# Other slots for the weight preparation inside an attention loop: offsets 0, 14, 23 in place of 0, 10, 18

## The chip, the core and the metric

The kernel runs on one core of a Trainium2 chip: TensorE (PE; its weight loads are told apart as PEld), VectorE (DVE), ScalarE (ACT), GpSimd (POOL) and SyncE (SP), which here issues nearly all DMAs. Time is device time in microseconds (us). The kernel before takes 1760.26 us, the median of three runs (1758.9 to 1764.62).

## The reference

It is one transformer block, whose inputs and outputs are float32. Its attention reads a cache; only the last 512 of the cached keys count.

```python
h = _layernorm(x) * (1 + ca) + sa                    # x: 2048 x 512
q = h @ wq                                           # 32 heads of 128
scores = q k^T * Dh ** -0.5                          # 8 kv heads, last 512 keys
x = x + ga * (softmax(scores) @ v) @ wo
h = _layernorm(x) * (1 + cb) + sb
x = x + gb * ((_gelu(h @ w_gate) * (h @ w_up)) @ w_down)   # F = 1792
```

## The kernel before

**Arithmetic.** Each float32 operand is split into two float16 halves, a high and a low part, and a product is three matmuls (`mm3`, lines 85 to 87: high by high, high by low, low by high). The projections and the feed-forward products (FFN) use seven block products in place of eight, so their weights are needed as sums and differences of blocks too, each again split in two halves.

**The loop.** The attention is one loop over T = 512 slots, written out in Python. A slot t is one scoring tile of 128 rows by 512 keys. Four slots are a unit (one head on one block of 512 rows). In slot t the program writes down, in this order: the three scoring matmuls of tile t on PE (`scores`, into one of two banks `ps`); the row maximum on DVE (`peak`, L943, `nm<-ps`); the low half of the probabilities of tile t-3 on DVE (`low`, L971) with their DMA transpose on SP (L975, `pt<-p`); the exponential of tile t on ACT (`expo`, L952, `ee<-ps,nm`); the high half of tile t-2 on ACT (L966); then about three groups of matmuls of other work (query projection `qa`, `qb`, `qc`, probabilities by values `po`, output projection `py`). All engines keep this written order: nothing is reordered by a scheduler. Since there are two `ps` banks, the scoring matmuls of tile t wait for the exponential of tile t-2.

**The weight preparation.** At the end of a slot stands what a table of positions puts there. In the second half of the loop this is, among other things, the preparation of the FFN weights, in seven rounds n = 0 to 6 of 30 slots each, which begin at slot b = 286 + 30 n. A round is for a pair of FFN tiles and has three parts:

- `prep_set(2n, b)` for the gate weights and `prep_set(2n+1, ...)` for the up weights. Each loads two tiles of float32 weights (`rw<-in_wg`, `rw<-in_wu`); at offsets 1 and 2 from the part's begin ACT takes their sums of squares (`sumsq`, L216, `junk<-rw`); at offset 4 a small matmul (L220) and a chain of column operations make a scale from them (`f_spread`); at offsets 7, 9, 10, 11 and 12 POOL scales the tiles, makes the sums and differences, and splits them into staging tiles (L160, L156, L157, L1360), and SP stores each three slots after (`kept<-stage`).
- `prep_wd(n, ...)` for the down weights, in the same way: loads `raw<-in_wd`, sums of squares at its offsets 0 and 1, the scale at 4, POOL's work at 7, 9, 11, 12 and 13 (L156, L157, L1413; DVE scales first, L1410), stores three slots after.

**Buffers and loads.** The `rw` tiles have two buffers, the `raw` and staging tiles five together. A planner goes through all loads in order of their first use. It wants a load three slots before that use (AHEAD), but not before the buffer that it takes is free by the table (its last use plus one slot), and if that is later than the use itself, it puts the load into the slot of the use:

```python
go = pos[0] - ahead
free = released[kind].pop(0) + LDGAP
pending[kind].append((max(min(max(go, free), pos[0]), 0), max(free + 3, pos[0] - 9), load))
```

SP issues in the written order. A load whose buffer is still being read waits on SP, and what stands behind it on SP waits too.

Of the kernel before, what the change touches and what calls it, by code (L numbers as in the profile page):

```python
# [62 lines left out]
def block_kernel(ctx: ExitStack, tc: tile.TileContext, x, kT, v, wq, wo, wg, wu, wd, cT, wc, wm, out):  # L63
# [11 lines left out]
    def raw(name):  # L75
        return pool.tile([P, 512], F32, tag="raw", name=name, bufs=NRAW)
# [14 lines left out]
    def dma(out_, in_):  # L91
        moved[0] += 1
        nc.sync.dma_start(out_, in_)
# [58 lines left out]
    def halves(dst, src, act=False):  # L152
        if act:
            nc.scalar.activation(dst[:, 0, :], src, AF.Copy)
        else:
            nc.gpsimd.tensor_scalar(dst[:, 0, :], src, 1.0, 1.0, op0=ALU.mult, op1=ALU.mult)  # L156
        nc.gpsimd.tensor_tensor(dst[:, 1, :], src, dst[:, 0, :], op=ALU.subtract)  # L157

    def times(t, by):
        nc.gpsimd.tensor_scalar(t, t, by, 1.0, op0=ALU.mult, op1=ALU.mult)  # L160
# [15 lines left out]
    def col(name, i=0):  # L176
        return ST[name][:, i:i + 1]
# [7 lines left out]
    def little(name, n=1, bufs=4, dtype=F32):  # L185
        return small.tile([P, n], dtype, tag=name, name=name, bufs=bufs)
# [27 lines left out]
    def sumsq(out, src):  # L214
        with nc.allow_low_precision(reason="only a scale follows from it, which the margin in norm2 covers"):
            nc.scalar.activation(junk, src, AF.Square, scale=PRE, accum_out=out)  # L216
# [75 lines left out]
    def f_spread(i, m):  # L292
        w = little("lw", 1, 2)
        norm2(w, m, 2, 1.0 / TOP13)
        pool_ts(col("finv", i), w, col("mf"))
        pool_ts(col("tsc", i), col("finv", i), GELU_A * GELU_C)
        then(lambda: nc.vector.reciprocal(col("fsc", i), w))
# [24 lines left out]
    def store(key, t, slack=6):  # L322

        KEPT[key] = dram.tile(list(t.shape), F16, name="kept")
        if slack and 0 <= now[0] < T - 8:
            bg.append((now[0] + slack, now[0], len(KEPT), lambda: dma(KEPT[key], t)))
        else:
            dma(KEPT[key], t)
# [225 lines left out]
    def sched(pos, ld, *more, kind="raw", ahead=AHEAD, lane="w"):  # L554
        loads.append(((pos,) + more, ld, kind, ahead, lane))
# [164 lines left out]
    def set_load(key, srcs, only=None):  # L720
        for k, src in enumerate(srcs):
            if only in (None, k):
                t = pool.tile([P, 512], F32, tag="rw", name="rw", bufs=NRW)
                dma(t, src)
                RAW.setdefault(key, {})[k] = t

    def pair_stat(key, m, k):
        if not m:
            m["m"] = little("lm", 4, dtype=BF16)
        sumsq(m["m"][:, k:k + 1], RAW[key][k])  # L730
# [35 lines left out]
    def plain_steps(key, by):  # L766
        def part(k):
            SET.setdefault(key, [None, None])[k] = get_w(k)
            times(RAW[key][k], by)
            halves(SET[key][k], RAW[key][k])  # L770

        return lambda: part(0), lambda: part(1)
# [386 lines left out]
    for g in range(NG):  # L1159
# [6 lines left out]
        if 0 < g < GW:  # L1166
            a, b = plain_steps(g, by)
            sched_pair(g, srcs, t0 - (19 if g > 1 else 13), spread, [(t0 - (13 if g > 1 else 8), a)], [(t0 - (11 if g > 1 else 7), b)])
        elif g >= GW and (not half or pr < GW):
            sched_set(g, srcs, t0, by, spread)  # L1170
            if not half:
                a, b, c, d, e, f = SETPOS2 if g == GW else SETPOS
# [32 lines left out]
    def set_srcs(q):  # L1205
        n, m = divmod(q, 2)
        f = 2 * (n % NP)
        return [(wg, wu)[m][f], (wg, wu)[m][f + 1]]

    def f_scale(q):  # L1210
        return (q // 2) % NP * 2 + q % 2
# [133 lines left out]
    def staged():  # L1345
        box = {}

        def alloc():
            box["t"] = pool.tile([P, 2, 512], F16, tag="raw", name="stage", bufs=NRAW)

        return box, alloc

    def prep_set(q, b):
        m, key, by = {}, ("f", q), col("fsc", f_scale(q))
        l, r = slice(0, 256), slice(256, 512)
        outs = [staged() for _ in range(4)]
        srcs = set_srcs(q)

        def tt(o, a, c, op):
            nc.gpsimd.tensor_tensor(o, a, c, op=op)  # L1360

        def made(k, src):
            halves(outs[k][0]["t"] if k < 3 else outs[k][0]["t"][:, :, 0:256], src)

        def keep_it(k):
            return lambda: store(("w", key, k), outs[k][0]["t"] if k < 3 else outs[k][0]["t"][:, :, 0:256], 0)

        def s0():
            times(RAW[key][0], by)
            made(0, RAW[key][0])  # L1370

        def s1():
            r1 = RAW[key][1]
            times(r1, by)
            made(3, r1[:, r])
            tt(r1[:, r], r1[:, l], r1[:, r], ALU.add)

        def s2():
            r0, r1 = RAW[key][0], RAW[key][1]
            tt(r1[:, l], r0[:, l], r1[:, l], ALU.subtract)  # L1380
            tt(r0[:, l], r1[:, r], r0[:, l], ALU.subtract)
            tt(r0[:, r], r0[:, r], r0[:, l], ALU.subtract)

        sched(b + 1, (lambda: set_load(key, srcs, 0), [lambda: pair_stat(key, m, 0), nop]), b + 11, kind="rw")
        sched(b + 2, (lambda: set_load(key, srcs, 1), [lambda: pair_stat(key, m, 1), lambda: f_spread(f_scale(q), m["m"]), s2, nop]),
              b + 4, b + 10, b + 12, kind="rw")
        sched(b + 7, (outs[0][1], [s0, keep_it(0)]), b + 10)
        sched(b + 9, (outs[3][1], [s1, keep_it(3)]), b + 12)
        sched(b + 11, (outs[1][1], [lambda: made(1, RAW[key][0]), keep_it(1)]), b + 14)
        sched(b + 12, (outs[2][1], [lambda: made(2, RAW[key][1]), keep_it(2)]), b + 15)  # L1390

    def prep_wd(n, b):
        m, st = {}, {}
        outs = [staged() for _ in range(4)]
        l, r = slice(0, 256), slice(256, 512)

        def load(k):
            st[k] = raw("raw")
            dma(st[k], wd[(2 * n + k) * P:(2 * n + k + 1) * P, :])

        def stat(k):
            if not m:
                m["m"] = little("lm", 4, dtype=BF16)
            sumsq(m["m"][:, k:k + 1], st[k])

        def spread():
            d_spread(n, m["m"])

        def scaled(k):
            nc.vector.scalar_tensor_tensor(st[k], st[k], col("dsc", n), rows[5], op0=ALU.mult, op1=ALU.mult)  # L1410

        def minus(o, a, b):
            nc.gpsimd.tensor_tensor(st[o[0]][:, o[1]], st[a[0]][:, a[1]], st[b[0]][:, b[1]], op=ALU.subtract)  # L1413

        def more():
            st[2] = raw("raw")

        def s0():
            scaled(0)
            halves(outs[0][0]["t"], st[0])  # L1420

        def s1():
            scaled(1)
            halves(outs[1][0]["t"], st[1])

        def s2():
            minus((2, l), (1, r), (1, l))
            minus((2, r), (0, r), (2, l))
            minus((0, r), (0, r), (1, r))
            minus((0, l), (0, l), (2, r))  # L1430

        def keep_it(k):
            return lambda: store(("wd", n, k), outs[k][0]["t"], 0)

        sched(b, (lambda: load(0), [lambda: stat(0), nop]), b + 13)
        sched(b + 1, (lambda: load(1), [lambda: stat(1), spread, nop]), b + 4, b + 11)
        sched(b + 7, (outs[0][1], [s0, keep_it(0)]), b + 10)
        sched(b + 9, (outs[1][1], [s1, keep_it(1)]), b + 12)
        if n < NP - 1:
            sched(b + 11, (more, [s2, nop]), b + 13)  # L1440
            sched(b + 12, (outs[2][1], [lambda: halves(outs[2][0]["t"], st[2]), keep_it(2)]), b + 15)
            sched(b + 13, (outs[3][1], [lambda: halves(outs[3][0]["t"], st[0]), keep_it(3)]), b + 16)

    at(T // 2 + 34, lambda: mod_row(5))
    for n in range(NP):
        b = T // 2 + 30 + 30 * n
        prep_set(2 * n, b)
        prep_set(2 * n + 1, b + 10)
        prep_wd(n, b + 18)
    for k in range(2):  # L1450
        at(T - 1 + 2 * k, lambda k=k: WO.update({("f", 0, k): fetch(("wd", 0, k), get_wo())}))
    for q, ps_ in ((0, (T - 18, T - 17, T - 16, T - 15)), (1, (T - 8, T - 7, T - 3, T)), (2, (T + 2, T + 3, T + 4, T + 5))):
# [242 lines left out]
    for i in range(QT):  # L1695
        load, stat, norm, sub, alloc, high, low, turn = ln_pair(3, i, lambda k, i=i: y1_row(2 * QT + QT * k + i))
        b = 26 + 16 * i
# [16 lines left out]
    for q in range(NQ):  # L1714
        n, m = divmod(q, 2)
# [54 lines left out]
```

## Time and profile before

| | us |
|---|---|
| median of three runs (lowest, highest) | 1760.26 (1758.9, 1764.62) |
| the profiled execution | 1758.56 |
| its span, first to last instruction | 1756.8 |
| busy PE, DVE, ACT, POOL | 1715.1, 1485.1, 1218.3, 1001.9 |

The granted TensorE clock is 0.996 of full speed over the span. A matmul of 512 columns is drawn 0.38 us long, but the next one starts 0.22 us after it, since matmuls overlap; a loss on PE is therefore read from starts. The attention loop runs from about 24 us to about 1340 us of the span, and rounds 0 to 6 of the weight preparation from about 742 us to about 1300 us.

### The profile page before, as it was taken

What the parts mean: (1) busy time and instruction counts of PE and PEld (TensorE: products, weight loads), DVE (VectorE), ACT (ScalarE), POOL (GpSimd) and SP (SyncE); (2) the same over time, 40 slices, a digit from 0 to 9 for tenths busy, and PEclk for the clock granted to TensorE, in tenths of its full rate; (3) what the DMA queues carried; (4) which work ended last, traced back from release to release, by engine and by line L of the source; (5) the groups of instructions that cost most, each with busy time, mean ns of one, the idle gap of its engine ahead of it and who ended that gap; (6) DMA issues with size and microseconds to landing.
All of it is one profiled execution on the core that took longest, in us unless ns stands there. A gap on an engine that the chain in (4) does not pass through costs nothing.

```text
span 1756.8 us, 26455 instructions
## 1 busy us (share of the span) xinstructions
PE 1715.1 (98%) x8264; PEld 810.2 (46%) x8266; DVE 1485.1 (85%) x2552; ACT 1218.3 (69%) x2731; POOL 1001.9 (57%) x1210
## 2 busy tenths in 40 slices
PE   7999999999999999999999999999999999999998
PEld 4444444444444444444444434444444444445556
DVE  8888898989999898988897978889786688878776
ACT  6987888888878777778777777778775244445542
POOL 3999668787887834547476566467521432214431
PEclk9999999999999999999999999999999999999999
DMA  6989999999999988999999999899997444454331
GB/s 211 231 189 224 214 230 212 233 218 213 228 206 235 228 187 177 201 196 220 204 229 198 232 184 221 197 206 223 210 211 175 162 126 127 116 167 145 105 123 49
DMA packets 698349, 336.56 MB, mean 192 GB/s; under 512 B 597473, under 2 KB 612065, under 8 KB 698209
## 3 DMA queue, kind: packets, MB, share of 16 engines
q1 hardware_dynamic: 697920, 334.36, 84.1%
q8 instruction: 65, 1.06, 0.3%
q14 instruction: 76, 0.61, 0.1%
q10 hardware_dynamic: 288, 0.52, 0.1%
HBM read 132.78 MB, written 56.75 MB: 108 GB/s over the span
## 4 chain that ended last, share of the span: by engine, by line
PE 80%; DVE 9%; DMA 3%; ACT 3%; POOL 3%; issue 2%; SPq 1%; POOLq 0%; ACTq 0%; DVEq 0%
PE py L87 6%; PE py L86 6%; PE py L85 6%; PE ps L85 5%; PE ps L87 5%; PE ps L86 5%; PE po L87 5%; PE po L85 5%; PE po L86 5%; PE fa L85 3%; PE fa L87 3%; PE fa L86 3%; PE qa L85 2%; PE qa L87 2%; DVE p L971 2%; PE qa L86 2%
## 5 line engine op out<-in xcount | busy, mean ns | idle before, releaser
L952 ACT ACTIVATE ee<-ps,nm 128x512 f32<-128x512 f32 x512 | 350.3, 684 | 237.0 <-DVE nm L943 233.4
L971 DVE SCALAR_TENSOR_TENSOR p<-ee,rr,p 128x512 f16<-128x512 f32 x512 | 457.5, 894 | 21.0 <-ACT p L966 20.6
L943 DVE TENSOR_REDUCE nm<-ps 128x1 f32<-128x512 f32 x512 | 350.1, 684 | 108.6 <-PE ps L87 105.8
L966 ACT ACTIVATE p<-ee,rr 128x512 f16<-128x512 f32 x512 | 362.7, 709 | 1.8 <-DMA pt<-p 1.8
L85 PE MATMUL ps<-k,qt 128*128 128x512 f16 x512 | 194.4, 380 | 22.1 <-ACT ee L952 21.1
L85 PE MATMUL po<-pt,v 128*128 128x512 f16 x512 | 194.1, 379 | 3.8 <-DMA pt<-p 3.1
L87 PE MATMUL ps<-k,qt 128*128 128x512 f16 x512 | 194.8, 381 | 0.6 <-DVE qt L682 0.6
L87 PE MATMUL po<-pt,v 128*128 128x512 f16 x512 | 194.2, 379 | 0.9 <-POOL v L157 0.8
L86 PE MATMUL ps<-k,qt 128*128 128x512 f16 x512 | 194.8, 380 | 0.0
L87 PE MATMUL py<-wo,ot 128*128 128x512 f16 x512 | 194.2, 379 | 0.0
L86 PE MATMUL py<-wo,ot 128*128 128x512 f16 x512 | 194.2, 379 | 0.0
L86 PE MATMUL po<-pt,v 128*128 128x512 f16 x512 | 194.2, 379 | 0.0
L85 PE MATMUL py<-wo,ot 128*128 128x512 f16 x512 | 194.2, 379 | 0.0
L1239 POOL TENSOR_TENSOR fg<-fg 128x512 f32<-128x512 f32 x24 | 36.5, 1520 | 132.3 <-ACT sq L1278 56.5
L87 PEld LDWEIGHTS <-w 128*128 128x128 f16 x728 | 71.3, 98 | 86.6 <-issue 1.5
L86 PEld LDWEIGHTS <-w 128*128 128x128 f16 x728 | 71.4, 98 | 84.6 <-issue 2.6
L85 PEld LDWEIGHTS <-w 128*128 128x128 f16 x728 | 71.4, 98 | 83.5 <-issue 1.4
L952 ACT ACTIVATION_READ_ACCUMULATOR ee<-ps,nm 128x1 f32 x512 | 99.2, 194 | 0.0
L233 POOL TENSOR_TENSOR lw<-lw,half__86 128x1 f32<-128x1 f32 x37 | 21.8, 589 | 135.4 <-DVE lw L183 135.4
L500 POOL TENSOR_TENSOR turn<-xs,turn 128x512 f16<-128x512 f32 (+1 forms) x48 | 56.8, 1184 | 63.1 <-ACT turn L497 62.9
L682 DVE SCALAR_TENSOR_TENSOR ot<-po,ot 128x512 f16<-128x512 f32 x128 | 86.2, 673 | 7.6 <-ACT ot L681 7.1
L892 DVE SCALAR_TENSOR_TENSOR acc<-py,ysc,acc 128x512 f32<-128x512 f32 x112 | 82.8, 739 | 10.9 <-PE py L87 10.9
(321 smaller groups left out, 4044.1 us busy)
## 6 DMA issues: line engine op xcount, KB each, us to landing
w<-kept SPq DMA_DIRECT2D x123, 256.0 KB, 3.2
kept<-stage SPq DMA_DIRECT2D x68, 256.0 KB, 2.9
wo<-kept SPq DMA_DIRECT2D x65, 256.0 KB, 3.5
raw<-in_wo SPq DMA_DIRECT2D x56, 256.0 KB, 3.4
kept<-w SPq DMA_DIRECT2D x39, 256.0 KB, 3.4
rw<-in_wq SPq DMA_DIRECT2D x38, 256.0 KB, 3.1
pt<-p SPq DMA_TRANSPOSE x512, 3.5
kept<-wo SPq DMA_DIRECT2D x32, 256.0 KB, 2.9
```

The lines of the kernel that those rows point to most:

```text
L85: nc.tensor.matmul(ps, lhi, rhi, start=first, stop=False, skip_group_check=chain)
L86: nc.tensor.matmul(ps, lhi, rlo, start=False, stop=False, skip_group_check=chain)
L87: nc.tensor.matmul(ps, llo, rhi, start=False, stop=last, skip_group_check=chain)
L233: nc.gpsimd.tensor_tensor(out, out, half_, op=ALU.pow)
L500: nc.gpsimd.tensor_tensor(S[s][:, :, 1, :], side(s), S[s][:, :, 0, :], op=ALU.subtract)
L682: return lambda: nc.vector.scalar_tensor_tensor(t[:, 1, :], src, scale, t[:, 0, :], op0=ALU.mult, op1=ALU.subtract)
L892: nc.vector.scalar_tensor_tensor(acc[ti], st["p"], by, acc[ti], op0=ALU.mult, op1=ALU.add)
L943: nc.vector.tensor_reduce(nm, E[t]["ps"], axis=AX.X, op=ALU.max, negate=True)
L952: nc.scalar.activation(e, E[t]["ps"], AF.Exp, bias=E[t]["nm"], scale=1.0, accum_out=sm[:, t % 2:t % 2 + 1])
L966: nc.scalar.activation(p16[:, 0, :], E[t]["e"], AF.Copy, scale=E[t]["r"])
L971: nc.vector.scalar_tensor_tensor(p16[:, 1, :], E[t]["e"], E[t]["r"], p16[:, 0, :], op0=ALU.mult, op1=ALU.subtract)
L1239: nc.gpsimd.tensor_tensor(o, a, b, op=op)
```

## The change

Two offsets change, in the only place that calls the three parts:

```diff
     for n in range(NP):
         b = T // 2 + 30 + 30 * n
         prep_set(2 * n, b)
-        prep_set(2 * n + 1, b + 10)
-        prep_wd(n, b + 18)
+        prep_set(2 * n + 1, b + 14)
+        prep_wd(n, b + 23)
```

No operation is added, removed or altered. The second set's sums of squares move from slots 11 and 12 of a round to 15 and 16, its POOL work from 17 to 22 to 21 to 26; the down part's sums of squares move from 18 and 19 to 23 and 24, its POOL work from 25 to 31 to 30 to 36, which is slot 0 to 6 of the next round. The planner then places the loads anew.

First, SP in round 3 (b = 376), slots 11 to 13, where the up weights are loaded. `p16_...` is the probability tile that a DMA transpose reads; each slot has one transpose. Before:

```order
L975 DMA_TRANSPOSE pt_12888<-p16_12863 128x8x128
L93 DMA rw_12901<-in_wu 128x512
L975 DMA_TRANSPOSE pt_12888<-p16_12894 128x8x128
L93 DMA rw_12940<-in_wu 128x512
L93 DMA kept_12944<-stage_12723 256x1x256
L975 DMA_TRANSPOSE pt_12888<-p16_12927 128x8x128
```

With the change, slots 12 to 14:

```order
L975 DMA_TRANSPOSE pt_12881<-p16_12887 128x8x128
L93 DMA rw_12931<-in_wu 128x512
L93 DMA kept_12935<-stage_12741 256x1x256
L975 DMA_TRANSPOSE pt_12881<-p16_12918 128x8x128
L93 DMA rw_12966<-in_wu 128x512
L975 DMA_TRANSPOSE pt_12881<-p16_12953 128x8x128
```

The two loads move one slot down on SP, from slots 11 and 12 to 12 and 13.

Second, ACT at the first sum of squares that reads these loads. Before, slots 10 (its end) and 11:

```order
L966 ACTIVATE p16_12863<-ee_12800,rr_12827 128x512
L952 ACTIVATE ee_12890,sm_12861<-ps_12880,nm_12884 128x512
L956 ACTIVATE rr_12892<-sm_12861 128x2
L966 ACTIVATE p16_12894<-ee_12825,rr_12827 128x512
L681 ACTIVATE ot_12899<-po_12865 128x512
L216 ACTIVATE junk_90,lm_12912<-rw_12901 128x512
L952 ACTIVATE ee_12924,sm_12925<-ps_12914,nm_12918 128x512
```

With the change, slots 13 to 15:

```order
L952 ACTIVATE ee_12949,sm_12916<-ps_12939,nm_12943 128x512
L956 ACTIVATE rr_12951<-sm_12916 128x2
L966 ACTIVATE p16_12953<-ee_12883,rr_12885 128x512
L681 ACTIVATE qt_12955<-qd_12945,qsc_111 128x512
L952 ACTIVATE ee_12979,sm_12980<-ps_12969,nm_12973 128x512
L966 ACTIVATE p16_12982<-ee_12915,rr_12951 128x512
L821 ACTIVATE s1_12991<-qa_12984 128x512
L952 ACTIVATE ee_13011,sm_12980<-ps_13001,nm_13005 128x512
L956 ACTIVATE rr_13013<-sm_12980 128x2
L966 ACTIVATE p16_13015<-ee_12949,rr_12951 128x512
L681 ACTIVATE ot_13026<-po_12993 128x512
L216 ACTIVATE junk_90,lm_13031<-rw_12931 128x512
```

Before, load and sum of squares stand in the same slot, 11; now the sum of squares stands in slot 15, three slots behind its load. The same holds in all seven rounds. The down part's loads stand three to seven slots ahead of their use with the change (three before).

Third, POOL at the seam of rounds 3 and 4, where the down part of round 3 ends (`stage<-raw`) and the gate part of round 4 begins (`rw<-rw,fsc`). Before:

```order
L156 TENSOR_SCALAR stage_13490<-raw_13044 128x512
L157 TENSOR_TENSOR stage_13490<-raw_13044,stage_13490 128x512
L500 TENSOR_TENSOR turn_13590<-xs_12724,turn_13590 128x2x256
L233 TENSOR_TENSOR lw_13657<-lw_13657,half__86 128x1
L237 TENSOR_SCALAR lw_13657<-lw_13657 128x1
L237 TENSOR_SCALAR finv_116<-lw_13657,mf_124 128x1
L237 TENSOR_SCALAR tsc_117<-finv_116 128x1
L160 TENSOR_SCALAR rw_13404<-rw_13404,fsc_115 128x512
L156 TENSOR_SCALAR stage_13654<-rw_13404 128x512
L157 TENSOR_TENSOR stage_13654<-rw_13404,stage_13654 128x512
```

With the change:

```order
L237 TENSOR_SCALAR tsc_117<-finv_116 128x1
L1413 TENSOR_TENSOR raw_13641<-raw_13188 128x256
L1413 TENSOR_TENSOR raw_13641<-raw_13159,raw_13641 128x256
L1413 TENSOR_TENSOR raw_13159<-raw_13159,raw_13188 128x256
L1413 TENSOR_TENSOR raw_13159<-raw_13159,raw_13641 128x256
L156 TENSOR_SCALAR stage_13642<-raw_13641 128x512
L157 TENSOR_TENSOR stage_13642<-raw_13641,stage_13642 128x512
L156 TENSOR_SCALAR stage_13643<-raw_13159 128x512
L157 TENSOR_TENSOR stage_13643<-raw_13159,stage_13643 128x512
L160 TENSOR_SCALAR rw_13442<-rw_13442,fsc_115 128x512
L156 TENSOR_SCALAR stage_13644<-rw_13442 128x512
L157 TENSOR_TENSOR stage_13644<-rw_13442,stage_13644 128x512
```

Before, the down part's last split stood in slot 1 of round 4, six slots ahead of the gate part's first scaling in slot 7. Now its differences and splits stand in slots 4 to 6, directly ahead of that scaling, behind the column operations of the gate part's scale.

## The prediction, on record before the run

> **What bounds the kernel now.** First the page, then stretches of it: does PE, the busiest engine, lose time, and where? The columns of the second view are the stretch, its length, and busy time of PE, weight loads, DVE, ACT and POOL with counts of instructions, then granted clock, DMA share and GB/s.
>
> ```profile
> PE 1715.1 (98%) x8264; PEld 810.2 (46%) x8266; DVE 1485.1 (85%) x2552; ACT 1218.3 (69%) x2731; POOL 1001.9 (57%) x1210
> ...
> 200.00:600.00 400.00, 399.97 (x1879) 181.63 (x1878) 364.66 (x655) 328.40 (x784) 316.85 (x413) 1.00 1.02 222
> 740.00:1310.00 570.00, 549.88 (x2540) 247.56 (x2539) 487.61 (x846) 429.93 (x1009) 335.08 (x423) 0.99 0.98 211
> ```
>
> Early in the attention loop (200 to 600) PE never rests, though DVE, ACT, POOL and the DMAs are busier there than later. From 740 to 1310, the rounds of the weight preparation, PE rests for 570.00 - 549.88 = 20.1 us. How much slower is the loop there? One exponential is one slot, so I count them in the groups by line of the two stretches:
>
> ```profile
> L952 ACT ACTIVATE ee<-ps,nm 128x512 f32<-128x512 f32 x159 | 108.9, 685 | 67.7 <-DVE nm L943 66.5
> ...
> L952 ACT ACTIVATE ee<-ps,nm 128x512 f32<-128x512 f32 x217 | 148.4, 684 | 99.2 <-DVE nm L943 98.1
> ```
>
> A slot takes 400 / 159 = 2.516 us where PE is full. 217 slots would take 546 us; they took 570, so 24 us are lost, give or take a slot at the edges. The waits of the same stretch say to whom (total, times, longest):
>
> ```profile
> PE ps L85 <- ACT ee L952: 19.3, 8, 4.4
> PE po L85 <- DMA pt<-p: 0.4, 1, 0.4
> PE qa L85 <- ACT u L821: 0.3, 1, 0.3
> ...
> ACT junk L216 <- DMA rw<-in_wu: 35.4, 10, 5.9
> ACT junk L216 <- DMA raw<-in_wd: 0.2, 1, 0.2
> ```
>
> PE waits for the exponentials, and ACT waits 35.4 us for one kind of load: the up weights `rw<-in_wu`, which feed the second set's sums of squares. The gate weights' loads (`rw<-in_wg`) and the down weights' cost nothing or 0.2. One stall in full, round 3, engine by engine from the timeline (start, length, engine, line):
>
> ```profile
> 1013.51 1.62 POOL L157 TENSOR_TENSOR stage<-rw,stage 128x512 f16<-128x512 f32 x1
> 1015.80 1.15 POOL L157 TENSOR_TENSOR stage<-rw,stage 128x512 f16<-128x512 f32 x1
> ...
> 1015.16 0.34 SPq L93 DMA_DIRECT2D rw<-in_wu  x1
> 1016.98 0.48 SPq L93 DMA_DIRECT2D rw<-in_wu  x1
> ...
> 1011.44 0.58 ACT L681 ACTIVATE ot<-po 128x512 f16<-128x512 f32 x1
> 1017.90 0.63 ACT L216 ACTIVATE junk<-rw 128x512 f16<-128x512 f32 x1 [5.88 <-DMA rw<-in_wu]
> 1018.53 0.67 ACT L952 ACTIVATE ee<-ps,nm 128x512 f32<-128x512 f32 x1
> ...
> 1014.60 0.38 PE L87 MATMUL py<-wo,ot 128*128 128x512 f16 x1
> 1019.34 0.41 PE L85 MATMUL ps<-k,qt 128*128 128x512 f16 x1 [4.36 <-ACT ee L952]
> ```
>
> POOL ends its reading of the first `rw` buffer at 1013.51 + 1.62 = 1015.13; SP issues the load at 1015.16; it lands as ACT starts the sum at 1017.90. ACT had been free since 1011.44 + 0.58 = 1012.02. The exponential stands behind the sum, and PE, which may be two tiles ahead, runs dry. So the stall is a load whose buffer comes free about when its reader wants the data. It is on the path that sets the end: PE is full before and after, and nothing later can return its loss.
>
> **The change part by part.** No operation is added or removed. The one thing that decides is the distance between the load and the sum.
>
> *The wait on ACT.* The buffer is freed by the same POOL instruction as before (slot 11 of the first set, which stays). The sum moves four slots back, 4 x 2.516 = 10.1 us. The longest wait was 5.88, so that data which came 5.88 late now lie ready 10.1 - 5.88 = 4.2 us early. On SP the load stands one transpose further down; one slot, 2.5 us, if that ever decides, still leaves 1.7 us. The second load is freed at 1015.80 + 1.15 = 1016.95, issued at 1016.98 and read a slot later than the first, with the same room. The landing times of all `rw` loads are
>
> ```profile
> DMA to landing us min/median/max: 2.7/3.2/4.3
> ```
>
> so that a slow one costs 1.1 us more than a median one and fits too. ACT's wait goes to nothing.
>
> *What PE gets back.* Not 35.4 us: about 2 us of each wait are absorbed, since PE may run ahead. I count on PE. The waits for `ee` are 19.3 us in 8 pieces. Idle time is drawn from the modelled end, 0.38 us after a start, where the next matmul would have started after 0.22, so each piece hides 0.16: 8 x 0.16 = 1.3. The wait for `u`, in the wake of round 6's stall, is 0.3 + 0.16 = 0.45. To this comes a clock loss: after the three longest waits the matmuls start at half pace for a while.
>
> ```profile
> 781.31 0.59 PE L85 MATMUL ps<-k,qt 128*128 128x512 f16 x1 [3.48 <-ACT ee L952]
> 784.15 0.38 PE L86 MATMUL qa<-T,w 128*128 128x512 f16 x1
> ...
> 938.28 0.59 PE L85 MATMUL ps<-k,qt 128*128 128x512 f16 x1 [3.21 <-ACT ee L952]
> 941.14 0.38 PE L86 MATMUL qc<-C,w 128*128 128x512 f16 x1
> ...
> 1022.95 0.39 PE L85 MATMUL po<-pt,v 128*128 128x512 f16 x1
> ...
> 1014.60:1023.00 8.40, 4.04 (x12) 1.43 (x11) 2.28 (x5) 5.07 (x13) 3.47 (x4) 0.80 0.65 150
> 1100.00:1170.00 70.00, 70.00 (x329) 31.63 (x328) 65.66 (x116) 55.25 (x130) 40.33 (x54) 1.00 0.92 208
> ```
>
> Seven matmuls start from 781.31 until 784.15: 2.84 us where 7 x 0.216 = 1.51 would do, 1.33 lost. Seven from 938.28 until 941.14: 1.35. Nine from 1019.34 until 1022.95: 3.61 - 1.94 = 1.67. The granted clock is 0.80 in the last of these stretches and 1.00 where PE is full. Sum: 19.3 + 1.3 + 0.45 + 4.35 = 25.4 us, and the slots counted 24.
>
> *What the moves cost.* The same POOL, DVE, ACT and DMA work falls on other slots. The new place is the seam, where the down part of one round (POOL in slots 30 to 36) now runs straight into the gate part of the next (37 to 42). Its price in POOL time, from the groups of 740 to 1310:
>
> ```profile
> L1413 POOL TENSOR_TENSOR raw<-raw 128x256 f32<-128x256 f32 x24 | 22.5, 947 | 0.9
> L156 POOL TENSOR_SCALAR stage<-raw 128x512 f16<-128x512 f32 x26 | 17.7, 683 | 28.3 <-DVE raw L1410 28.3
> L157 POOL TENSOR_TENSOR stage<-raw,stage 128x512 f16<-128x512 f32 x26 | 33.7, 1297 | 2.2
> L160 POOL TENSOR_SCALAR rw<-rw,fsc 128x512 f32<-128x512 f32 x28 | 24.6, 879 | 32.3 <-issue 14.9 <-DVE fsc L297 10.4 <-ACT qt L681 3.8
> L156 POOL TENSOR_SCALAR stage<-rw 128x512 f16<-128x512 f32 x42 | 30.2, 720 | 2.6
> L157 POOL TENSOR_TENSOR stage<-rw,stage 128x512 f16<-128x512 f32 x42 | 54.7, 1303 | 3.5
> ```
>
> Slots 34 to 37 hold 4 x 0.947 + 2 x (0.683 + 1.297) + 0.879 + 0.720 + 1.303 = 10.7 us of POOL work in 4 x 2.516 = 10.1 us, and slot 38 holds none: POOL gets 0.6 us late and catches up. Its products are stored three slots (7.5 us) after they are written down, and in round 1 alone the second layer norm's differences fall on the same slots. POOL's whole load would be 335.08 / (570 - 25) = 61%, against 316.85 / 400 = 79% at 200 to 600, where PE lost nothing. So below, nothing; above, a wait like the one for a transpose in the view of the waits, 0.4 us and its hidden 0.16, in each of six seams and at each of the seven moved sets: 13 x 0.56 = 7.3 us. I take 0.5 us for all rounds together, near the lower end, for the stretch at 200 to 600 is the nearest row and denser. The 0.4 us wait for a transpose is left in.
>
> Against its own time: 1758.56 - 25.4 + 0.5 = 1733.7. The median of the runs lies 1.7 above the profiled execution: **1735.4 us**, 1.4% faster.
>
> **The rivals.** *The stall moves in part* to the seam, by way of SP. The store of a late POOL product waits on SP, and the transposes `pt<-p` behind it come late, for which PE waits (`po`). For it: one transpose (`pt<-p`, 0.4 us) is waited for already. Against it: POOL's lateness of 0.6 us against 7.5 us until the store. Price: a wait of 1 to 3 us in six rounds, 2 on the mean, 12 us: 1747.
>
> *The change doesn't do what it says*: the loads come as late as before since POOL or SP hold them, or ACT's pause was only the place where another shortage showed. For it: DVE is 65.66 / 70 = 94% busy in the clean stretch from 1100 to 1170, so PE could wait for `nm` next. Against it: that stretch contains a gate part's and a down part's sums, at the load distance of three slots which the second set now gets, and PE is busy for 70.00 of 70. Price: 25 us not won, 1760.
>
> *Slower, by DVE at the seam.* A DVE operation takes longer when POOL reads at the same time: the low halves `p` take 0.74 us alone and up to 1.83.
>
> ```profile
> L971 DVE SCALAR_TENSOR_TENSOR p<-ee,rr,p x218: 725/744/1826, 739.4 to 1308.8; 128x512 f16<-128x512 f32 x109
> ...
> L971 DVE SCALAR_TENSOR_TENSOR p<-ee,rr,p 128x512 f16<-128x512 f32 x218 | 191.7, 879 | 20.6 <-ACT p L966 20.6
> L971 DVE SCALAR_TENSOR_TENSOR p<-ee,rr,p 128x512 f16<-128x512 f32 x159 | 146.1, 919 | 0.0
> ```
>
> If unbroken POOL work made each `p` of the seam's 13 slots take 1.83 in place of the mean 0.879, DVE would need 0.95 us more a slot, with 0.155 free (6% of 2.516): 0.79 x 13 = 10.3 late, less 2 absorbed, 8.3 in each of six seams, 50 us: 1735 + 50 = 1785. It decides (over 1760) from 4.2 us a seam, a `p` of about 1.5 us throughout. Against it: at 200 to 600, with POOL at 79%, `p` takes 0.919 on the mean (last row), and PE is full. [...]
>
> **How the numbers follow.** Forecast 0.80; stall moved in part 0.12; no gain 0.05; slower 0.03. Forecast and partial move are faster by over 0.3% (5.3 us, about what a measurement of this kernel can tell): 0.92; the second rival is the same: 0.05; slower 0.03. The range: below, the lowest run, 1758.9, less all 26 us that PE lost, with a spread of 1.5: 1731. Above, the 7.3 us bound of the moves and the 4.4 us by which the highest run lies over the median: 1746, which takes in nearly half of the partial case.
>
> **What would show it.** Right: L216 waits for `rw<-in_wu` fall from 35.4 us to under 2; the waits of `ps` for `ee` between 740 and 1310 from 19.3 to under 2; PE's busy share of that stretch is near 100%, and no granted clock below 1.00 stands in it. The exponentials count 216 or so in 545 us. Wrong: ACT still waits at L216, or PE waits for `po` (SP late at the seam), or for `ee` behind long `nm` waits (DVE). Each step would then be off by what that wait shows.

## The result, and the profile after

The changed kernel takes 1735.72 us (median of four runs, 1734.66 to 1736.88) against 1760.74 for the kernel before in the same comparison (1758.9 to 1764.62): a ratio of 0.9855, with a 95% interval of 0.9837 to 0.9873. Its profiled execution took 1735.50 us (span 1733.7), 23.1 us less than that of before.

The page of the changed kernel, first busy time and share of PE, weight loads, DVE, ACT and POOL:

```profile
PE 1709.0 (99%) x8266; PEld 809.7 (47%) x8266; DVE 1485.3 (86%) x2552; ACT 1218.6 (70%) x2731; POOL 1001.8 (58%) x1210
```

The work of DVE, ACT and POOL is the same to 0.3 us; PE's drawn busy time is 6 us less, and no matmul of the rounds starts at half pace any more: the granted clock is 1.00 without a break from 18 to 1731 us, where before it was 0.50 for 3.41 us three times in the rounds. Then the stretch of the weight preparation, cut to 740 to 1285 so that the shorter loop fills it too, of before (first fence) and of the changed kernel (second):

```profile
740.00:1285.00 545.00, 524.88 (x2424) 236.20 (x2423) 466.90 (x810) 412.14 (x968) 331.09 (x419) 0.99 0.98 211
```

```profile
740.00:1285.00 545.00, 541.70 (x2528) 245.48 (x2526) 483.54 (x840) 428.10 (x1006) 335.21 (x423) 1.00 1.03 219
```

PE rested for 20.1 us of these 545; it now rests for 3.3. The groups of the changed kernel in the same stretch, for the exponentials and the low halves:

```profile
L952 ACT ACTIVATE ee<-ps,nm 128x512 f32<-128x512 f32 x216 | 147.9, 685 | 102.7 <-DVE nm L943 101.2
L971 DVE SCALAR_TENSOR_TENSOR p<-ee,rr,p 128x512 f16<-128x512 f32 x216 | 190.5, 882 | 2.0 <-ACT p L966 2.0
```

216 exponentials in 545 us are 2.52 us a slot, the pace of the clean stretches. And the waits there (total, times, longest):

```profile
ACT p L966 <- DMA pt<-p: 6.5, 5, 3.2
ACT junk L216 <- DMA rw<-in_wu: 3.3, 2, 2.9
...
PE po L85 <- issue: 1.3, 1, 1.3
PE po L85 <- DMA pt<-p: 1.2, 1, 1.2
...
PE ps L85 <- ACT ee L952: 0.7, 2, 0.5
```

ACT's wait for the up weights falls from 35.4 to 3.3 us, PE's wait for the exponentials from 19.3 to 0.7. Read from starts, the changed kernel gets through 2963 matmuls between 700 and 1340, where before got through 2864: 99 x 0.216 = 21.4 us. The other 1.7 us of the 23.1 lie outside this stretch, where the change moves nothing.

**Round 3, where the stall is gone.** From the timeline of the changed kernel:

```profile
1007.25 1.16 POOL L157 TENSOR_TENSOR stage<-rw,stage 128x512 f16<-128x512 f32 x1
1008.43 0.34 SPq L93 DMA_DIRECT2D rw<-in_wu  x1
...
1013.39 0.57 ACT L681 ACTIVATE ot<-po 128x512 f16<-128x512 f32 x1
1013.86 0.61 ACT L216 ACTIVATE junk<-rw 128x512 f16<-128x512 f32 x1
```

The landing times of the `rw` loads of the cut stretch:

```profile
DMA to landing us min/median/max: 2.8/3.3/5.7
```

The load still goes out as soon as POOL lets its buffer go (1007.25 + 1.16 = 1008.41, issued at 1008.43). With the median landing time it is there at 1011.7, 2.1 us before ACT, without a pause, takes the sum (the 5.7 us are a load of gate weights; this round's two up loads took 3.3 us at most).

**Round 2, where something is left.** POOL, SP, ACT and PE from the timeline of the changed kernel:

```profile
907.78 0.57 POOL L233 TENSOR_TENSOR lw<-lw,half__86 128x1 f32<-128x1 f32 x1 [2.08 <-DVE lw L183]
...
916.24 1.53 POOL L487 TENSOR_TENSOR xs<-xs 128x256 f32<-128x256 f32 x2
...
933.83 1.71 POOL L157 TENSOR_TENSOR stage<-rw,stage 128x512 f16<-128x512 f32 x1
...
935.57 0.34 SPq L93 DMA_DIRECT2D rw<-in_wu  x1
...
938.44 0.63 ACT L216 ACTIVATE junk<-rw 128x512 f16<-128x512 f32 x1 [2.94 <-DMA rw<-in_wu]
...
905.16 0.38 PE L85 MATMUL po<-pt,v 128*128 128x512 f16 x1 [1.26 <-issue]
...
939.88 0.38 PE L85 MATMUL ps<-k,qt 128*128 128x512 f16 x1 [0.21 <-ACT ee L952]
...
943.42 0.38 PE L85 MATMUL ps<-k,qt 128*128 128x512 f16 x1 [0.50 <-ACT ee L952]
...
948.01 0.38 PE L85 MATMUL po<-pt,v 128*128 128x512 f16 x1 [1.19 <-DMA pt<-p]
```

The four rests of PE here, 1.26 + 0.21 + 0.50 + 1.19 = 3.2 us, are all that the waits name in the stretch. The first has no releaser that the profile shows, and lies ahead of the load. The others follow a load that comes 2.9 us late in spite of the four slots: POOL lets its buffer go only at 933.83 + 1.71 = 935.54. From 907.7 until then it works almost without a gap:

```profile
907.70:935.60 27.90, 27.90 (x131) 12.60 (x129) 22.83 (x40) 22.62 (x51) 26.26 (x31) 1.00 0.91 190
```

And one of its groups there:

```profile
L487 POOL TENSOR_TENSOR xs<-xs 128x256 f32<-128x256 f32 x4 | 3.3, 836 | 0.2
```

26.26 of 27.90 us, among them the second layer norm's differences (L487), which fall on no other seam.

### The profile page after: what moved, and what is told of

Read it like the earlier page. It is cut to its first block, busy times and chain, and to the rows that moved or that the text cites. A ratio compares the mean times of both kernels' runs of the same rounds, so it can differ in the third digit from the quotient of the medians.

```text
span 1733.7 us, 26470 instructions
## 1 busy us (share of the span) xinstructions
PE 1709.0 (99%) x8266; PEld 809.7 (47%) x8266; DVE 1485.3 (86%) x2552; ACT 1218.6 (70%) x2731; POOL 1001.8 (58%) x1210
## 3 DMA queue, kind: packets, MB, share of 16 engines
q8 instruction: 65, 1.06, 0.3%
## 4 chain that ended last, share of the span: by engine, by line
PE 93%; DVE 3%; DMA 2%; ACT 1%; issue 1%; SPq 0%; POOL 0%; ACTq 0%; DVEq 0%; POOLq 0%
PE py L85 8%; PE py L86 8%; PE py L87 8%; PE po L85 6%; PE po L87 6%; PE ps L85 6%; PE po L86 6%; PE ps L87 6%; PE ps L86 6%; PE qa L87 3%; PE qa L86 3%; PE qa L85 3%; PE fa L85 3%; PE fa L87 3%; PE fa L86 3%; PE qc L87 1%
## 5 line engine op out<-in xcount | busy, mean ns | idle before, releaser
L85 PEld LDWEIGHTS <-v 128*128 128x128 f16 x524 | 51.2, 98 | 70.4 <-issue 9.8
```

Of the source, the lines that this page charges most:

```text
L85: nc.tensor.matmul(ps, lhi, rhi, start=first, stop=False, skip_group_check=chain)
```

## The experiments

All are read in the same stretch, 740 to 1285. Offsets are written (second set, down part): before (10, 18), changed (14, 23).

**Is it the late load? (places as before, the sums read a tile long in place.)** The second set's two sums of squares read other data, so that the up weights' real scale is left out. The first of the two lines, and what takes its place (`...` marks what is left out here):

```diff
-        sched(b + 1, (lambda: set_load(key, srcs, 0), [lambda: pair_stat(key, m, 0), nop]), b + 11, kind="rw")
...
+        def stat(k):
+            if q % 2 == 0:
+                return pair_stat(key, m, k)
...
+                nc.scalar.activation(junk, rows[2], AF.Square, scale=PRE * 40.0, accum_out=m["m"][:, k:k + 1])
...
+        sched(b + 1, (lambda: set_load(key, srcs, 0), [lambda: stat(0), nop]), b + 11, kind="rw")
```

> All places as in the kernel before, but the second set's two sums of squares read a tile that has been in place for long and not the loaded up weights, so the real scale of the up weights is left out. ACT does the same work at the same place and no longer waits for the load; the load itself stays in the slot where it was. Theory: no wait of ACT at the sum, PE loses about 1 us in the stretch, 1735 us. Rival (another shortage at this place): PE loses 10 us or more there, 1745 us or above.

Measured: 1733.88 us (1733.1 to 1735.54), ratio 0.985 (0.9832 to 0.9868). The stretch:

```profile
740.00:1285.00 545.00, 544.83 (x2545) 247.25 (x2543) 489.36 (x848) 431.17 (x1011) 334.40 (x423) 1.00 1.03 221
```

PE's one wait for an exponential there:

```profile
PE ps L85 <- ACT ee L952: 0.2, 1, 0.2
```

With every instruction in its old slot and the loads issued on POOL's release as before (in round 3 at 1004.21, when the sum that no longer needs them has run since 1003.69), the whole loss goes. The late load is the cause, and nothing else in the old places costs PE more than 0.2 us in the stretch. It also shows about how much the places can give: the changed kernel, whose PE rests for 3.3 us, is 1.8 us above it.

**How far must the sum move? One slot: (11, 18).**

```diff
-        prep_set(2 * n + 1, b + 10)
+        prep_set(2 * n + 1, b + 11)
```

> Second set at offset 11, the down part at 18 as before: the sums of squares stand one slot later, at 12 and 13, and nothing else of the change is made. Theory (distance from freed buffer to reader): each round's first wait of ACT for the up weights falls by one slot, 2.5 us, from 5.12, 3.77, 5.16, 5.88, 3.92, 4.47 and 4.97 us to 15.7 us in all. PE absorbs about 2 us of each, so that it loses some 3 us in the stretch of the seven rounds, and the time is about 1738 us. Rival (the wait is only where another shortage shows): the time stays at 1750 us or above, with PE waiting for something else.

Measured: 1755.8 us (1752.43 to 1759.44), ratio 0.9973 (0.9961 to 0.9985). The waits:

```profile
ACT junk L216 <- DMA rw<-in_wu: 31.9, 10, 5.3
...
PE ps L85 <- ACT ee L952: 14.1, 11, 2.5
```

The first sum of round 1 on the engines that it needs, from the timeline:

```profile
850.19 1.56 POOL L157 TENSOR_TENSOR stage<-rw,stage 128x512 f16<-128x512 f32 x1
852.37 0.71 ACT L966 ACTIVATE p<-ee,rr 128x512 f16<-128x512 f32 x1
853.72 1.38 SPq L975 DMA_TRANSPOSE pt<-p  x1
855.19 0.53 SPq L93 DMA_DIRECT2D rw<-in_wu  x1
858.34 0.63 ACT L216 ACTIVATE junk<-rw 128x512 f16<-128x512 f32 x1 [5.26 <-DMA rw<-in_wu]
```

The stretch:

```profile
740.00:1285.00 545.00, 528.74 (x2451) 238.52 (x2449) 476.27 (x820) 415.39 (x977) 331.63 (x421) 1.00 0.99 213
```

A miss: my arithmetic of "one slot is 2.5 us of room" gave most of the gain, but the time is 4 us below that of before, not 22, and ACT's wait fell by 3.5 us in 35.4. The load had moved with its reader. The planner puts a load whose buffer comes free no earlier than the slot of its use into that slot; the sum in slot 12 has its load in slot 12, as the sum in slot 11 had it in slot 11. Here the buffer was free at 851.75, but SP issues in the written order, and the load stands behind the slot's transpose, which ends at 855.10. So the data is there at the later of POOL's release and SP's own place, plus some 3 us (3.1 and 3.6 for this round's two), and a reader in the load's own slot waits for it even when the buffer is free. It is so in six of the seven rounds: the first load goes out 1.9 to 3.8 us after its buffer is free, and only in round 3 within 0.4 us.

**Two slots: (12, 18).**

```diff
-        prep_set(2 * n + 1, b + 10)
+        prep_set(2 * n + 1, b + 12)
```

> Second set at offset 12, the down part at 18: the sums of squares stand at 13 and 14, the loads at 12 and 13, one slot ahead by the table. Theory: ACT's waits fall by two slots, 5.0 us each, to about 1 us in all, and PE loses nothing to them: 1735 us, though the load stands one slot ahead and not three. Rival (a load needs its three slots): the waits stay above 10 us and the time above 1740 us.

Measured: 1737.27 us (1735.64 to 1738.04), ratio 0.9865 (0.9844 to 0.9886). Its waits:

```profile
ACT junk L216 <- DMA rw<-in_wu: 18.0, 13, 2.3
PE ps L85 <- ACT ee L952: 3.3, 6, 1.1
```

Now the load stays in slot 12 and the sum is in 13. This one slot of distance brings nearly all of the gain. ACT still waits for 18.0 us, far more than the 1 us that I expected (and above the 10 that the rival named, whose time of 1740 us did not come), but in 13 pieces of at most 2.3, and PE, which may run two tiles ahead, feels 3.3 of it. How much PE takes up differs from wait to wait: of the seven first waits before, 1.4 us (3.92, of which PE felt 2.49) to 3.3 (4.97, felt as 1.67); here 2.23 us is felt as 1.06 and 2.32 not at all.

**The second set alone: (14, 18)**, run twice.

```diff
-        prep_set(2 * n + 1, b + 10)
+        prep_set(2 * n + 1, b + 14)
```

> The second set alone at 14, the down part at 18 as before. Theory (after the first four runs: a wait of ACT is the later of POOL's release and SP's own place, plus the landing, and the seam of down part and next gate part makes POOL late): with the load three slots ahead and no seam, ACT waits under 2 us for the up weights, PE loses 1 to 2 us in the stretch of the rounds, about 1734 us. Rival (the down part had to move as well, for its POOL work now overlaps that of the second set in slots 25 and 26): PE loses 5 us or more, 1738 us or above.

> The second set alone at 14 again, for its first run came out at 1739.5 us, while its profile had lost only 3.7 us in the stretch of the rounds. If the time is from the places of the work: again 1738 to 1740 us, and the profile shows where outside the stretch PE loses 2 us or more against (14, 21). If it was chance: 1735 to 1737 us.

Measured: 1739.46 us (1738.23 to 1739.84), ratio 0.988 (0.9864 to 0.9897), and the second time 1739.31 (1737.41 to 1740.99), 0.9883 (0.9862 to 0.9903), while the changed kernel on the same chip took 1736.28. From the second:

```profile
PE po L85 <- DMA pt<-p: 3.0, 1, 3.0
PE ps L85 <- ACT ee L952: 1.6, 3, 0.9
```

No sum waits for the up weights, yet it is 3 us slower than with both moves, where I expected 1734: a second miss. Its profiled execution, the lowest of its four runs (1737.41), lies 1.4 above the changed kernel's (1736.03), and PE's rests in the stretch account for that: 545 - 540.40 = 4.6 against 545 - 541.76 = 3.2. The wait of 3.0 us stands at 908.00, in the same slot of round 2 in which PE of the changed kernel rests for 1.3 without a releaser, and where it rests in no kernel whose layer norm is moved (below). Its other runs are up to 3.6 us longer. They have a lower mean granted clock, 0.998, 0.997 and 0.997 against 0.999, and at half pace 0.001 of the clock is 1.7 us of 1737 (an estimate); so a clock loss goes with the longer times, but where it falls in those runs no profile shows. In the profile of the first comparison (1738.23 us) one falls at 94 to 98 us, far ahead of the rounds, where the clock is 0.57.

**The down part alone: (10, 23).**

```diff
-        prep_wd(n, b + 18)
+        prep_wd(n, b + 23)
```

> The down part alone at 23, the second set at 10 as before. Theory: ACT waits 33 to 36 us for the up weights as before, and the time is that of before, 1760 us, or up to 4 us above, if what the changed kernel loses in round 2 comes from the seam of down part and next gate part. Rival (the down part's move gives part of the gain): 1755 us or below.

Measured: 1783.81 us (1781.69 to 1786.67), ratio 1.0133 (1.0113 to 1.0154): 24 us slower, where I expected 1760 to 1764. The stretch:

```profile
740.00:1285.00 545.00, 509.49 (x2317) 227.95 (x2316) 442.30 (x776) 395.19 (x926) 307.74 (x397) 0.97 0.94 201
```

The waits:

```profile
ACT junk L216 <- DMA rw<-in_wu: 53.5, 11, 11.7
...
PE ps L85 <- ACT ee L952: 35.5, 7, 9.3
```

Round 2 from the timeline:

```profile
944.33 1.15 POOL L157 TENSOR_TENSOR stage<-rw,stage 128x512 f16<-128x512 f32 x1
945.50 0.34 SPq L93 DMA_DIRECT2D rw<-in_wu  x1
948.56 0.63 ACT L216 ACTIVATE junk<-rw 128x512 f16<-128x512 f32 x1 [11.74 <-DMA rw<-in_wu]
```

This is the third miss, and the telling one. The seam that I had priced at next to nothing makes POOL late for the *same* buffer. The first wait of each round, before and with the down part moved:

| round | 0 | 1 | 2 | 3 | 4 | 5 | 6 |
|---|---|---|---|---|---|---|---|
| before | 5.12 | 3.77 | 5.16 | 5.88 | 3.92 | 4.47 | 4.97 |
| (10, 23) | 5.06 | 6.68 | 11.74 | 6.98 | 5.66 | 7.82 | 6.42 |

Round 0, which has no seam ahead of it, is unchanged. In the others ACT waits longer by 2.9, 6.6, 1.1, 1.7, 3.3 and 1.5 us, and in all six the load goes out 0.03 us after POOL's release. So the two offsets can't be judged apart: the down part's move costs 24 us while the sum stands in the slot of its load, and gains 3 us beside the second set's move (1739.31 against 1736.28, from (14, 18) to (14, 23)). The granted clock of 0.97 in the stretch, after 0.99, adds to the price: PE's waits for the exponentials, seven of up to 9.3 us, grow by 16 us, the time by 24. In the trace of before, half pace follows the three longest waits, 3.21, 3.48 and 4.36 us: the clock is 0.50 for 3.41 us around the end of each, and matmuls start 0.43 us apart in place of 0.22. It can follow a shorter one too. At (11, 18):

```profile
1016.34 0.54 PE L85 MATMUL ps<-k,qt 128*128 128x512 f16 x1 [2.55 <-ACT ee L952]
...
1016.50:1020.00 3.50, 3.50 (x10) 1.24 (x9) 2.43 (x5) 3.14 (x9) 0.00 (x0) 0.52 0.22 50
```

The same wait of about 2.5 us cost no clock twice in the kernel before (2.49 and 2.46, with a clock of 1.00 and starts 0.22 us apart behind them), so after a wait of that length it does not follow every time.

**Down part at 21: (14, 21)**, run twice.

```diff
-        prep_wd(n, b + 23)
+        prep_wd(n, b + 21)
```

> Second set at 14, down part at 21: its POOL work, slots 28 to 34, lies behind the second set's and ends three slots ahead of the next gate part's. Theory: the 3.9 us that the changed kernel loses in round 2 go, since POOL is no longer late at the next gate part; PE loses about 1 us in the stretch, 1733 us. Rival (the loss in round 2 has another cause than the seam): 1735.5 us, as with the change.

> Second set at 14, down part at 21, again. Theory: ACT waits for no load of the up weights, PE loses 1 to 3 us in the stretch, and the time lies 1 to 3 us below that of (14, 23) on the same chip. Rival: no difference of the medians by more than 0.5 us.

Measured: 1734.89 us (1733.62 to 1735.49), ratio 0.9853 (0.9838 to 0.9867), and 1734.6 (1733.63 to 1735.38), 0.9853 (0.9836 to 0.9869). In the second, PE rests for 1.6 us:

```profile
740.00:1285.00 545.00, 543.44 (x2537) 246.50 (x2536) 487.22 (x845) 429.44 (x1009) 335.65 (x423) 1.00 1.03 220
```

No sum waits for the up weights. It lies about 1.7 us under the changed kernel on the same chip (1736.28, below); only the lowest run of that reaches into its range. My first expectation, 1733 us, was too low; the second, 1 to 3 us below the changed kernel, holds.

**Is round 2's rest the layer norm on the seam? (14, 23) with the second layer norm's steps eight slots later.**

```diff
-        plan_pair(2, 285 + 48 * i, i, lambda k, i=i: y1_row(QT * k + i))
+        plan_pair(2, 293 + 48 * i, i, lambda k, i=i: y1_row(QT * k + i))
```

> The changed kernel (14, 23) with the second layer norm's plan eight slots later, so that its differences on POOL (L487) fall no longer on the seam of rounds 1 and 2. Theory: round 2 then loses no more than the other rounds, ACT's longest wait for the up weights, 2.9 us there, goes to nothing, and PE loses 1 to 2 us in the stretch, about 1733 us. Rival (the seam itself suffices): round 2 still loses 2 us or more, 1735 us.

> The changed kernel (14, 23) again, beside three others on one chip. Theory: 1735 to 1736 us; its profile again has a late load of the up weights in round 2 (ACT waits 2 to 4 us there) and PE loses about 4 us in the stretch of the rounds, since the order that makes POOL late there is the program's. Rival (that loss was chance): less than 1.5 us lost there.

Measured: 1734.32 us (1732.85 to 1735.33), ratio 0.985 (0.9835 to 0.9865). The changed kernel, run again, took 1736.28 (1735.04 to 1736.89), 0.9862 (0.9845 to 0.9878), with the same waits as the first time (2.9 us at the sum, 1.3 and 1.2 on PE). With the layer norm away from the seam:

```profile
ACT junk L216 <- DMA rw<-in_wu: 0.8, 1, 0.8
PE po L85 <- DMA pt<-p: 0.7, 1, 0.7
PE ps L85 <- ACT ee L952: 0.4, 1, 0.4
```

The 2.9 us wait of round 2 is gone, the wait without a releaser at 905.16 too, and what the waits of PE name falls from 3.2 to 1.1 us. So the layer norm on the seam is the cause of round 2's rest by the profile, together with the seam: at (14, 21), with the layer norm in its old place, no sum waits either. By the times it is likely but weaker: the two kernels ran in different comparisons, and their ranges overlap by 0.3 us. The run that overlaps is the profiled one (1735.33), and in its profile the clock falls to 0.51 from 94.0 to 97.5 us, far ahead of the rounds.

**Both: (14, 21) and the layer norm eight slots later.**

> Second set at 14, down part at 21, and the second layer norm's plan eight slots later: both ways of lightening POOL's work ahead of the next gate part together. Theory: nothing is left to win over either alone, 1733 to 1735 us, PE loses 1 to 2 us in the stretch. Rival (the two effects add up): 1 us or more below (14, 21).

Measured: 1732.83 us (1732.39 to 1734.13), ratio 0.9844 (0.9827 to 0.9861). The stretch:

```profile
740.00:1285.00 545.00, 544.69 (x2543) 247.05 (x2542) 486.88 (x848) 429.44 (x1010) 336.22 (x423) 1.00 1.02 221
```

Its waits:

```profile
ACT junk L216 <- DMA rw<-in_wu: 2.0, 1, 2.0
PE po L85 <- DMA pt<-p: 0.2, 1, 0.2
```

PE rests for 0.3 us of 545, as in the kernel whose sums wait for no load. On the same chip it is 3.4 us under the changed kernel (1736.28), with no run of either in the other's range, and so beats both kernels. I had expected it to bring nothing over either half alone; by the medians it is 1.8 us under (14, 21), though one of its four runs lies in that one's range. So the rival, that the two add up, fits better.

## Why the prediction was right, and where it was not

Forecast 1735.4, measured 1735.72, in the range of 1731 to 1746 and faster as given 0.92. By its steps:

- *What bounds the kernel.* Right. PE full early in the loop, and in the rounds a sum of squares that waits for a load: with that wait alone taken away, in the old places, PE rests for 0.2 us. Of the signs named, one fell short: ACT's waits for the up weights are 3.3 us, not under 2.
- *What PE gets back, 25.4 us.* Right in size: the kernel without the wait gains 1758.56 - 1733.60 = 25.0 us from profiled execution to profiled execution. The way of counting held too: the 35.4 us on ACT overstate the gain, the 19.3 drawn on PE understate it.
- *The wait on ACT, "4.2 us early".* This is the step that failed in part. That the buffer is freed by the same POOL instruction is true; that it is freed at the same time is not. The down part's move puts POOL behind: behind a seam ACT waits 1.1 to 6.6 us longer (the table of (10, 23) against before). Round 3 had 2.1 us left of the 4.2. Round 2, by its own wait of 5.16, would have had 10.1 - 5.2 = 4.9 us of room; less the 6.6 it is 1.7 late, and the trace has 2.9.
- *What the moves cost, 0.5 us.* The mis-sized term. PE rests for 3.3 us in the stretch against 0.2 without the wait, so it was about 3 us, inside the bounds of 0 to 7.3. The sum of POOL's work at the seam, 10.7 us in 10.1, left out two things. The gate part's column operations stand in the same slots; from the groups of the changed kernel:

```profile
L233 POOL TENSOR_TENSOR lw<-lw,half__86 128x1 f32<-128x1 f32 x21 | 12.5, 596 | 71.7 <-DVE lw L183 71.7
...
L237 POOL TENSOR_SCALAR lw<-lw 128x1 f32<-128x1 f32 x28 | 8.1, 291 | 2.4
L237 POOL TENSOR_SCALAR tsc<-finv 128x1 f32<-128x1 f32 x14 | 4.6, 330 | 1.2
L237 POOL TENSOR_SCALAR finv<-lw,mf 128x1 f32<-128x1 f32 x14 | 4.6, 326 | 1.4
```

  One of each is 1.5 us, which makes the lateness 2.1 us in place of 0.6; in the five rounds without the layer norm ACT's wait grew by 2.1 on the mean (2.9, 1.1, 1.7, 3.3, 1.5), so the size fits, though the single rounds scatter. And the layer norm was named for this seam but given no price; with it round 2's wait grew by 6.6. The comparison that kept the term low, with the denser stretch at 200 to 600, says that POOL's *load* costs PE nothing (POOL 79% busy there, PE for 399.97 of 400 us). It doesn't say when POOL lets a buffer go.
- *The sum.* 1733.7 was forecast for the profiled execution and 1735.50 measured, 1.8 us of gain missing. By medians the forecast came closer, because the median of before lay 1.7 us above its profiled execution when I added that distance, and the changed kernel's lies only 0.2 above its own. The median's hit is in part luck.
- *The stall moves in part by way of SP* (0.12). Only round 2 has anything like it, one wait of 1.19 us for a transpose, and there what stood on SP was the load whose buffer POOL still held, not a store. All of round 2's rests together are 3.2 us, not 12.
- *The change doesn't do what it says* (0.05). False here, but its reason, that loads are held by POOL or SP, is what (11, 18) shows at one slot.
- *Slower, by DVE at the seam* (0.03). In the cut stretch the low halves take 882 ns on the mean after 883 (724 to 1831 singly, before 725 to 1826), and ACT's waits for `nm` are 101.2 us for 216 slots after 91.3 for 207, 0.47 us a slot after 0.44. By single operations DVE does pay beside POOL's work, but not each time: every low half of 1.0 us or more, 52 in each of the two traces, ran beside it, the other 94 beside it stayed under 1.0 us in each trace, and none that ran apart from it (61 before, 70 now) took over 0.76 us. Packing that work closer did not make DVE pay for it more often.

## What to carry to other kernels

When a reader waits for a load, measure the distance between the two in the written order before the reader's place: a planner that takes the load along gives back little (4 us of 25 here), and the first slot of true distance gave nearly everything. When work is pushed together to make that room, add up all of the releasing engine's work in those slots, the small column operations and other tables' entries included, and ask when the buffer comes free, not only how busy the engine is. Judge two offsets of one table together, since a move that cost 24 us alone gained 3 beside the other.

## What was not expected of the hardware

PE feels little of many short waits on ACT: 18.0 us in 13 pieces of at most 2.3 cost 3.3 us drawn on PE at (12, 18), while 31.9 us in 10 pieces of up to 5.3 cost 14.1 at (11, 18). A wait of PE of 2.55 us, shorter than the 3.21 us after which it was seen before, can be followed by half pace (clock 0.52 for 3.5 us at (11, 18)), and a mean clock that reads 1.00 over 545 us hides it. And SP's written order can be the later of two gates: at (11, 18) the buffer was free at 851.75 and ACT at 853.08, but the load went out at 855.19, behind its slot's transpose, and ACT waited 5.26 us, no less than before.
